# A transformer kernel on one core: first Q chunks by pairs of token tiles, Wq loaded behind four x tiles instead of eight, and two layernorms moved

## The chip, the cores and the metric

The kernel runs on one core of one Trainium2 chip. The metric is the device time of one execution in microseconds (us); lower is better. Each kernel was executed several times; beside every changed kernel, the kernel before was run on the same chip.

The engines: PE is the matmul engine, PEld its weight loads, DVE the vector engine, ACT the scalar engine, POOL the general one, SP the engine from which most transfers (DMA) are issued.

## The reference, cut to what matters

Four blocks in sequence on x of 2048 tokens by 1024: attention, feed-forward, attention, feed-forward, each with a layernorm in front and a residual.

```python
def _A_ref(x, wqkv, wo):            # H = 32 heads, Dh = 32, window W = 8, dilation 2
    qkv = ... (x @ wqkv) ...
    logits = einsum("bhsd,bhswd->bhsw", q, kg) * scale    # 8 earlier keys per token
    o = einsum("bhsw,bhswd->bhsd", softmax(logits), vg)
    return o @ wo
def _B_ref(x, w1, b1, w2, b2):
    return gelu(x @ w1 + b1) @ w2 + b2
x = x + _A_ref(_layernorm(x), ...)
x = x + _B_ref(_layernorm(x), ...)
# and both once more
```

## The kernel before

Tokens are worked in four groups of 512 (four tiles of 128 tokens each). For a group, Q, K and V are each made in 8 chunks of 8 matmuls of 512 columns. DVE multiplies Q by shifted K ("products") and adds them up in trees; PE sums over the heads ("head sum"); softmax; DVE multiplies by shifted V ("averaging"); PE applies wo. Between layernorm and Q the normalised tile `xn` has to be transposed into `xnT`: for the first group on PE, for later groups by a DMA transpose. The parts that the argument touches:

```python
wpool = ... bufs=5            # weight tiles of 1 MB; two make Wq, two Wk, two Wv
xn = lnp.tile(..., name="xn", bufs=3)

load_x(0)                     # four x tiles of 256 KB, on the SP queue
...
def ln_first():               # first group
    s = [ln_stats(0)]
    for tt in range(NTT):
        if tt + 1 < NTT:
            s.append(ln_stats(tt + 1))
        xn = ln_norm(tt, *s[tt])
        transpose_on_pe(xn, xa[0][:, tt, :, :])
        warm_up(4)            # matmuls on zeros, to keep the matmul clock up

def gen_qkv(n, ...):
    wq = load_qkv(0)
    wk = load_qkv(1)
    for c in range(6 if n == 0 else 0):           # first half of k for six chunks
        first[c] = qkv_chunk(wq, c, xnT, None, 0, KD // 2)
    for c in range(NCH):
        ps = ...                                  # rest of the chunk
        act.copy(qT[:, c, :], ps[:]); yield
    wv = load_qkv(2)                              # emitted after the last Q chunk
    ...                                           # 8 K chunks, then 8 V chunks

ln_first()
load_x(1)
stage(gen_qkv(0, 2), sides=at(0, ln_a, 1) + at(8, load_x, 2) + at(12, load_x, 3) + at(14, load_bias)
      + at(19, head_sum, 0, False))
q1 = gen_qkv(1, 2, defer=True, qk_pool=early)
stage(q1, sides=at(2, attend, 0) + at(2, spread, 0) + at(2, hold) + at(2, ln_a, 2, early) + ...)
...
stage(gen_ffn2(0), sides=at(15, hold) + ... + at(23, hold) + at(23, ln_a, 3))
```

`at(u, f, n)` emits f(n) after the u-th chunk of a stage. A scheduler then orders the instructions of each engine, and each engine runs its own in that order. `hold` keeps DVE work that is emitted later from being moved ahead of what was emitted before.

## Time and profile before

Median 1246.09 us (1245.93 to 1246.15, four runs): very steady.

| | value | where it is read |
|---|---|---|
| span | 1244.3 us | page |
| PE busy | 1233.5 us, 99% | page, part 1 |
| granted matmul clock | 1.000 | cores |
| spacing of 512-column matmuls | 216 ns | start to start, from the records |
| first real matmul | 14.22 us | timeline |
| PE waits after that | about 2.6 us in sum | timeline, start to start less 216 ns |

```profile
PE 1233.5 (99%) x5785; PEld 630.8 (51%) x5835; DVE 835.2 (67%) x864; ACT 305.7 (25%) x475; POOL 99.1 (8%) x215
```

This is part 1 of the page: busy time, share of the span and number of instructions. With PE at 99% there is little to win, and where it is shows in the timeline of PE. The columns are start, busy time, engine, line, operation, output and inputs, shape and number of merged instructions; in brackets the idle time before them and what ended it.

```profile
14.22 26.06 PE L118 MATMUL acc<-xnT,wt 128*128 128x512 bf16 x120 [0.34 <-ACT xnT L93]
...
49.12 0.62 PE L118 MATMUL L<-big,smat 128*32 128x512 bf16 x8
...
62.44 0.62 PE L118 MATMUL L<-big,smat 128*32 128x512 bf16 x8 [0.46 <-DVE big L93]
...
100.47 31.27 PE L118 MATMUL acc<-xnT,wt 128*128 128x512 bf16 x144 [0.75 <-ACT vT L93]
...
152.40 0.62 PE L118 MATMUL L<-big,smat 128*32 128x512 bf16 x8
...
258.83 1.89 PE L118 MATMUL acc<-wt,oT 128*128 128x512 bf16 x8 [0.47 <-DVE tmp L93]
...
260.96 8.79 PE L118 MATMUL acc<-wt,oT 128*128 128x512 bf16 x39 [0.24 <-DVE x L93]
...
269.68 0.62 PE L118 MATMUL L<-big,smat 128*32 128x512 bf16 x8
```

The `L` lines are head sums. There are four places with waits: the head until 14.22, the second head sum at 62.44 (DVE's products), the third group's Q at 100.47, and the second wo at 258 to 261. The wait at 100.47 is put down to ACT, but the third group's last DMA transpose lands at 100.34.

The next lines are the SP queue of the same kernel in the first Q stage. `wt` at 22.80 and 28.08 are the two halves of Wv; transposes and x tiles stand between them. From the landings in the trace, Wv's halves arrive at 30.21 and 36.74 us, and V starts on PE near 42 us.

```profile
22.80 0.57 SPq L93 DMA_DIRECT2D wt<-in_A_wqkv_dram  x1
23.46 2.05 SPq L93 DMA_TRANSPOSE xnT<-xn  x1
25.57 2.41 SPq L93 DMA_DIRECT2D x<-in_A_x_dram  x4
28.08 0.60 SPq L93 DMA_DIRECT2D wt<-in_A_wqkv_dram  x1
```

### The profile page before, as it was taken

The numbers are of one execution on the slowest core, as the hardware profiler recorded it, in microseconds if no ns is written. First come the engines' busy times: TensorE is split into PE (matmuls) and PEld (weight loads), VectorE is DVE, ScalarE is ACT, GpSimd is POOL, SyncE is SP. The second block draws the span as 40 slices with busy tenths as digits, with TensorE's granted clock in tenths as the row PEclk, the third lists the DMA queues.
The fourth block names the chain that finished last, engine by engine and source line by source line (L and its number), as shares of the span: only waits on it lengthen the run. The fifth ranks groups of instructions, "written<-read, shape, count | busy, mean of one in ns | idle before, by whom it ended". The sixth has DMA issues, their size and how long they took to land.

```text
span 1244.3 us, 13978 instructions
## 1 busy us (share of the span) xinstructions
PE 1233.5 (99%) x5785; PEld 630.8 (51%) x5835; DVE 835.2 (67%) x864; ACT 305.7 (25%) x475; POOL 99.1 (8%) x215
## 2 busy tenths in 40 slices
PE   9999999999999999999999999999999999999998
PEld 5666544446444564445644456444554444444444
DVE  4999989896995989527994379943598688012001
ACT  3333252013430134201351013410234101310310
POOL 3040010012001100101001010000000002000000
PEclk9999999999999999999999999999999999999999
DMA  9755564466846647555566575566754567546441
GB/s 284 253 190 169 152 208 148 161 174 207 212 135 203 169 149 206 185 170 148 177 176 197 165 176 170 163 195 197 192 161 140 182 203 179 181 157 194 148 138 53
DMA packets 215295, 219.81 MB, mean 177 GB/s; under 512 B 66034, under 2 KB 184960, under 8 KB 212160
## 3 DMA queue, kind: packets, MB, share of 16 engines
q1 hardware_dynamic: 212560, 208.16, 56.0%
q0 software_dynamic: 2672, 10.76, 2.7%
q8 instruction: 45, 0.74, 0.2%
q14 instruction: 18, 0.15, 0.0%
HBM read 197.40 MB, written 6.29 MB: 164 GB/s over the span
## 4 chain that ended last, share of the span: by engine, by line
PE 79%; issue 0%; DVE 0%; POOL 0%
PE acc L118 78%; PE L L118 0%; DVE x L93 0%; POOL rstd L93 0%; DVE xn L93 0%
## 5 line engine op out<-in xcount | busy, mean ns | idle before, releaser
L118 PE MATMUL acc<-xnT,wt 128*128 128x512 bf16 x3328 | 722.1, 379 | 1.1 <-ACT vT L93 0.8
L118 PEld LDWEIGHTS <-wt 128*128 128x128 bf16 x3328 | 394.8, 119 | 325.2 <-issue 5.3
L118 PE MATMUL acc<-wt,hT 128*128 128x512 bf16 (+1 forms) x1780 | 386.0, 376 | 2.1
L118 PEld LDWEIGHTS <-hT 128*128 128x128 bf16 x1820 | 178.1, 98 | 209.0
L93 DVE TENSOR_TENSOR big<-big 128x2048 bf16<-128x2048 bf16 (+2 forms) x182 | 240.3, 1349 | 1.8
L93 ACT ACTIVATE hT<-acc,b1T 128x512 bf16<-128x512 f32 x224 | 151.6, 687 | 318.4 <-PE acc L118 317.8
L93 DVE TENSOR_TENSOR big<-abc,vT 128x4096 bf16<-128x4096 bf16 x64 | 144.2, 2282 | 52.1 <-DMA abc<-a_d 52.1
L93 DVE TENSOR_TENSOR big<-qT,kT 128x4096 bf16<-128x4096 bf16 x64 | 143.9, 2286 | 31.4 <-ACT kT L93 30.5
L93 DVE TENSOR_TENSOR tmp<-acc,b2bc 128x512 f32<-128x512 f32 x56 | 38.6, 689 | 178.8 <-PE acc L118 175.4
L93 ACT CAST qT<-acc 128x512 bf16<-128x512 f32 x64 | 37.2, 587 | 332.8 <-PE acc L118 332.7
L118 PE MATMUL acc<-wt,oT 128*128 128x512 bf16 x440 | 97.7, 379 | 1.1 <-DVE tmp L93 0.5
L93 DVE BATCH_NORM_STATS2 stats<-x 128x6 f32<-128x512 bf16 x128 | 83.9, 677 | 3.3 <-DMA x<-in_A_x_dram 2.5
L118 PEld LDWEIGHTS <-oT 128*128 128x128 bf16 x448 | 43.9, 98 | 53.8 <-issue 1.3
L93 DVE TENSOR_TENSOR x<-acc,big 128x512 bf16<-128x512 f32 (+1 forms) x9 | 5.7, 632 | 90.0 <-PE acc L118 90.0
L93 POOL TENSOR_TENSOR rstd<-mv,eps_t 128x1 f32<-128x1 f32 x64 | 19.0, 297 | 502.1 <-DVE mv L93 502.1
L93 ACT CAST vT<-acc 128x512 bf16<-128x512 f32 x64 | 37.5, 586 | 84.7 <-PE acc L118 84.7
L93 DVE TENSOR_SCALAR xn<-x,mv,rstd 128x1024 bf16<-128x1024 bf16 x64 | 34.8, 543 | 35.0 <-POOL rstd L93 30.9
L93 ACT CAST kT<-acc 128x512 bf16<-128x512 f32 x64 | 37.4, 586 | 70.5 <-PE acc L118 70.5
L93 POOL DMA_DIRECT2D a_d<-a x32 | 19.6, 637 | 411.7 <-DVE a L93 411.7
L93 DVE TENSOR_TENSOR x<-acc,x 128x512 bf16<-128x512 f32 x64 | 42.8, 671 | 2.6 <-PE acc L118 2.3
L93 POOL TENSOR_TENSOR rstd<-rstd,mhalf 128x1 f32<-128x1 f32 x64 | 40.6, 634 | 5.0
L93 DVE TENSOR_TENSOR x<-tmp,x 128x512 bf16<-128x512 f32 x56 | 38.6, 689 | 1.5
(48 smaller groups left out, 207.7 us busy)
## 6 DMA issues: line engine op xcount, KB each, us to landing
wt<-in_B_w_dram SPq DMA_DIRECT2D x56, 1024.0 KB, 5.8
wt<-in_B_w_dram SPq DMA_DIRECT2D x64, 896.0 KB, 4.9
wt<-in_A_wqkv_dram SPq DMA_DIRECT2D x48, 1024.0 KB, 5.6
wt<-in_A_wo_dram SPq DMA_DIRECT2D x16, 1024.0 KB, 5.0
abc<-a_d POOLq DMA_DIRECT2D x32, 256.0 KB, 4.2
x<-in_A_x_dram SPq DMA_DIRECT2D x16, 256.0 KB, 6.2
out_dram<-x SPq DMA_DIRECT2D x31, 128.0 KB, 1.8
a_d<-a POOLq DMA_DIRECT2D x32, 64.0 KB, 3.6
```

Of the source, the lines that this page charges most:

```text
L93: inst = f(*args, **kwargs)
L118: return pe(nc.tensor.matmul(*args, **kwargs))
```

## The change

Its intent is to take away all four waits: start Q on two tiles instead of four and fetch Wq sooner (the head); do the third group's layernorm and transposes early, and the first group's attention later (the waits at 62 and 100 us); take the statistics of the fourth group's layernorm out of the crowded place at 250 us (the wait at 258). The text below calls the three parts head, middle and statistics.

```diff
 # head
+wq_first = load_qkv(0)                       # right behind the first four x tiles
 def ln_first():
-    ... four tiles normalised, transposed on PE, 4 warm-ups each
+    ... tiles 0 and 1 transposed on PE, copied in halves, 4 warm-ups in all;
+    ... tiles 2 and 3 only normalised, their transposes put in first_late
 # in gen_qkv
-for c in range(6 if n == 0 else 0):
-    first[c] = qkv_chunk(wq, c, xnT, None, 0, KD // 2)
+for kh in range(2 if n == 0 else 0):
+    for c in range(6):
+        first[c] = qkv_chunk(wq, c, xnT, first.get(c), kh * (KD // 2), (kh + 1) * (KD // 2), 0, 2)   # tiles 0, 1: 256 columns
+        if kh == 1 and c in (0, 3):
+            transpose_on_pe(*first_late.pop(0))
 ...                                           # then tiles 2, 3 of each chunk
 # middle
-stage(gen_qkv(0, 2), sides=at(0, ln_a, 1) + at(8, load_x, 2) + at(12, load_x, 3) + at(14, load_bias)
+stage(gen_qkv(0, 2), sides=at(0, load_x, 2) + at(0, ln_a, 1) + at(1, load_x, 3) + at(6, ln_a, 2, early) + at(14, load_bias)
-stage(q1, sides=at(2, attend, 0) + at(2, spread, 0) + at(2, hold) + at(2, ln_a, 2, early) + ...
+stage(q1, sides=at(6, attend, 0) + at(6, spread, 0) + at(6, hold) + ...
 # statistics
-stage(gen_ffn2(0), sides=at(15, hold) + ... + at(23, ln_a, 3))
+stage(gen_ffn2(0), sides=at(0, ln_stats_ahead, 3) + at(15, hold) + ... + at(23, ln_a, 3, None, True))
```

The order of the SP queue before: x of groups 0 and 1, Wq, Wk, three transposes, Wv first half, one transpose, x of group 2, Wv second half, x of group 3. After: x of group 0, Wq, x of group 1, Wk, x of group 2, three transposes, half of group 3's x, a transpose, the other half, three transposes of the third group, Wv first half, a transpose, Wv second half.

More of the change, by code (lines that the diff above doesn't have):

```diff
@@ L127, with load_qkv @@
     load_x(0)
+    def load_qkv(which):
+        tiles = []
+        for h in range(2):
+            wt = wpool.tile([P, KD // 2, D], BF16, name="wt")
+            sp.dma_start(wt[:], wqkv_v[:, h * (KD // 2):(h + 1) * (KD // 2), which * D:(which + 1) * D])
+            tiles.append(wt)
+        return tiles
+    wq_first = load_qkv(0)
     warm = bigp.tile([P, P], BF16, name="big")
@@ L145 @@
     b2bc = const.tile([P, D], BF16, name="b2bc")
+    mv_ahead = const.tile([P, NTT, 2], F32, name="mv_ahead")
+    rstd_ahead = const.tile([P, NTT, 1], F32, name="rstd_ahead")
     def build_constants():
@@ L165, in load_bias, with ln_stats @@
         act.copy(b1T[:], ps[:])
-    def ln_stats(t):
+    def ln_stats(t, mv=None, rstd=None, between=None):
         stats = lnp.tile([P, 2, 6], F32, name="stats")
@@ L171, in ln_stats @@
             vec.bn_stats(stats[:, h, :], x[t][:, h * HALF:(h + 1) * HALF])
-        mv = lnp.tile([P, 2], F32, name="mv")
+            if h == 0 and between is not None:
+                between()
+        if mv is None:
+            mv = lnp.tile([P, 2], F32, name="mv")
+            rstd = lnp.tile([P, 1], F32, name="rstd")
         vec.bn_aggr(mv[:], stats[:])
-        rstd = lnp.tile([P, 1], F32, name="rstd")
         pool.tensor_tensor(out=rstd[:], in0=mv[:, 1:2], in1=eps_t[:], op=ALU.add)
@@ L177, in ln_stats, with ln_stats_ahead @@
         return mv, rstd
+    def ln_stats_ahead(g):
+        for tt in range(NTT):
+            ln_stats(g * NTT + tt, mv_ahead[:, tt, :], rstd_ahead[:, tt, :])
     def ln_norm(t, mv, rstd):
@@ L182, in ln_norm, with transpose_on_pe @@
         return xn
-    def transpose_on_pe(xn, out):
-        pst = psum.tile([P, KD, P], BF16, name="acc", bufs=6)
+    def transpose_on_pe(xn, out, pst=None, halves=1):
+        if pst is None:
+            pst = psum.tile([P, KD, P], BF16, name="acc", bufs=6)
         for k in range(KD):
             pe(nc.tensor.transpose(pst[:, k, :], xn[:, k * P:(k + 1) * P], ident[:]))
-        act.copy(out, pst[:])
+        n = KD // halves
+        for h in range(halves):
+            act.copy(out[:, h * n:(h + 1) * n, :], pst[:, h * n:(h + 1) * n, :])
     late = []
@@ L194, in transpose_late, with ln_tile @@
             transpose_on_pe(*late.pop(0))
-    def ln_tile(t, tt, xnT, on_pe=False):
-        mv, rstd = ln_stats(t)
+    def ln_tile(t, tt, xnT, on_pe=False, ahead=False):
+        mv, rstd = (mv_ahead[:, tt, :], rstd_ahead[:, tt, :]) if ahead else ln_stats(t)
         xn = ln_norm(t, mv, rstd)
@@ L202, in ln_tile @@
         sp.dma_start_transpose(xnT[:, tt, :, :], xn[:].rearrange("s (k p) -> s k p", p=P))
+    first_late = []
     def ln_first():
@@ L207, in ln_first, with norm @@
         vec.on = True
-        s = [ln_stats(0)]
-        for tt in range(NTT):
-            if tt + 1 < NTT:
-                s.append(ln_stats(tt + 1))
-            xn = ln_norm(tt, *s[tt])
-            transpose_on_pe(xn, xa[0][:, tt, :, :])
-            warm_up(4)
+        both = psum.tile([P, 2, KD, P], BF16, name="L", bufs=1)
+        stats = {}
+        def norm(tt):
+            xn = ln_norm(tt, *stats.pop(tt))
+            if tt < 2:
+                transpose_on_pe(xn, xa[0][:, tt, :, :], halves=2)
+            else:
+                first_late.append((xn, xa[0][:, tt, :, :], both[:, tt - 2, :, :]))
+            if tt == 0:
+                warm_up(4)
+        stats[0] = ln_stats(0)
+        stats[1] = ln_stats(1)
+        norm(0)
+        stats[2] = ln_stats(2, between=lambda: norm(1))
+        stats[3] = ln_stats(3, between=lambda: norm(2))
+        norm(3)
         vec.on = False
@@ L227, with qkv_chunk @@
     xb = {}
-    def load_qkv(which):
-        tiles = []
-        for h in range(2):
-            wt = wpool.tile([P, KD // 2, D], BF16, name="wt")
-            sp.dma_start(wt[:], wqkv_v[:, h * (KD // 2):(h + 1) * (KD // 2), which * D:(which + 1) * D])
-            tiles.append(wt)
-        return tiles
-    def qkv_chunk(wts, c, xnT, ps=None, k0=0, k1=KD):
+    def qkv_chunk(wts, c, xnT, ps=None, k0=0, k1=KD, t0=0, t1=NTT):
         if ps is None:
@@ L240, in qkv_chunk @@
         for k in range(k0, k1):
-            mm(ps[:], lhsT=wts[k // (KD // 2)][:, k % (KD // 2), c::NCH], rhs=xnT[:, :, k, :], start=(k == 0), stop=(k == KD - 1))
+            mm(ps[:, t0 * P:t1 * P], lhsT=wts[k // (KD // 2)][:, k % (KD // 2), c::NCH], rhs=xnT[:, t0:t1, k, :],
+               start=(k == 0 and t0 == 0), stop=(k == KD - 1), skip_group_check=t1 - t0 < NTT)
         return ps
@@ L282, in gen_qkv @@
         qk_pool = qk_pool or attp
-        wq = load_qkv(0)
+        wq = wq_first if n == 0 else load_qkv(0)
         wk = load_qkv(1)
@@ L286, in gen_qkv @@
         first = {}
-        for c in range(6 if n == 0 else 0):
-            first[c] = qkv_chunk(wq, c, xnT, None, 0, KD // 2)
+        for kh in range(2 if n == 0 else 0):
[3 more added lines that the diff above has]
+                    transpose_on_pe(*first_late.pop(0))
         for c in range(NCH):
-            ps = qkv_chunk(wq, c, xnT, first[c], KD // 2) if c in first else qkv_chunk(wq, c, xnT)
+            ps = qkv_chunk(wq, c, xnT, first[c], t0=2) if c in first else qkv_chunk(wq, c, xnT)
             act.copy(qT[:, c, :], ps[:])
@@ L436, in warm_up, with ln_a @@
             mm(ps[:], lhsT=warm[:], rhs=warm[:].unsqueeze(1).to_broadcast([P, NTT, P]), start=True, stop=True)
-    def ln_a(n, pool=None):
+    def ln_a(n, pool=None, ahead=False):
         xa[n] = new_xnT(pool)
         for tt in range(NTT):
-            ln_tile((n % NG) * NTT + tt, tt, xa[n])
+            ln_tile((n % NG) * NTT + tt, tt, xa[n], ahead=ahead)
     def stage(gen, count=None, sides=()):
@@ L471 @@
         load_x(1)
-        stage(gen_qkv(0, 2), sides=at(0, ln_a, 1) + at(8, load_x, 2) + at(12, load_x, 3) + at(14, load_bias)
-              + at(19, head_sum, 0, False))
+        stage(gen_qkv(0, 2), sides=at(0, load_x, 2) + at(0, ln_a, 1) + at(1, load_x, 3) + at(6, ln_a, 2, early)
+              + at(14, load_bias) + at(19, head_sum, 0, False))
         q1 = gen_qkv(1, 2, defer=True, qk_pool=early)
-        stage(q1, sides=at(2, attend, 0) + at(2, spread, 0) + at(2, hold) + at(2, ln_a, 2, early) + each(new_prod, 1, 8, 1, 0, 4) + each(av, 0, 12, 1))
+        stage(q1, sides=at(6, attend, 0) + at(6, spread, 0) + at(6, hold) + each(new_prod, 1, 8, 1, 0, 4) + each(av, 0, 12, 1))
         q2 = gen_qkv(2, defer=True)
@@ L481 @@
     stage(gen_ffn1(0), sides=at(2, attend, 1) + at(2, spread, 1) + at(2, hold) + each(new_prod, 2, 2, 1, 0, 4) + each(av, 1, 6, 2))
-    stage(gen_ffn2(0), sides=at(15, hold) + each(new_prod, 2, 15, 1, 4, 8) + at(23, hold) + at(23, ln_a, 3))
+    stage(gen_ffn2(0), sides=at(0, ln_stats_ahead, 3) + at(15, hold) + each(new_prod, 2, 15, 1, 4, 8) + at(23, hold) + at(23, ln_a, 3, None, True))
     for n in range(1, N - 2):
```

## The prediction

> **What bounds it now.** TensorE. On the page PE is busy 1233.5 of 1244.3 us (99%) at a granted clock of 1.000; the chain of waits is almost all PE matmuls, 216 ns start to start. The change can only win time in which PE has no useful work. The timeline shows where that is:
> - the head: the first real matmul starts at 14.22 us, after four token tiles are normalised and transposed;
> - 62.4 us: 0.5 us, PE waits for the last product tree before the first group's attention sums (DVE works without a break from 30.6 to 62.4);
> - 99.3 to 100.5: 0.9 us; put down to ACT, but the third group's last DMA transpose lands at 100.34, so I read it as xnT being late;
> - 258.0 to 261.4: about 1.2 us, wo waits for accumulators that DVE has not emptied, because the fourth group's layernorm (250.3 to 259.7) stands before the adds.
>
> **The change, costed.**
> 1. Head. The first six Q chunks start on tiles 0 and 1. The second tile's normalise can follow at about 8.1, its half copies end near 10. Wq lies behind four x tiles, not eight. In the trace 256 KB takes 0.67 us and 1 MB 2.70 us once the queue is full, and landings keep the order of issue (the Trainium skill, "DMA: Bandwidth & Descriptors", "Queues, rings and completion order", has each engine consume its ring in order; the trace agrees). x3 lands at 6.80; Wq's halves then land near 9.5 to 10.2 and 12.2 to 12.9 (12.87 and 15.58 before). First real matmul about 10.2. Splitting 48 matmuls into 96 of 256 columns is almost free: 109 ns apiece in the last FFN. The wait for tile 3 (copied near 16.7) takes some back: Q ends near 25.4, not 28.0. Gain 2.6 us.
> 2. Given back. x4 to x11 and Wk now lie ahead of the DMA transposes, and the third group's layernorm stands before the products on DVE and waits for xn buffers that transposes free. Products start about 30.5, as before, with one normalise inserted: first tree about 47.3 (46.5 before), needed after the fourth V chunk, which PE reached at 48.8 before. Wv's second half lies behind transposes: I estimate it lands near 41 (36.74 before), 1 us after V wants it. Either way 1.3 us is lost: net 1.3 us at the first head sum.
> 3. Attention of group 0 moves four Q chunks later: removes the 0.5 us wait; DVE idles instead. The wait at 99.3 (0.9 us) goes. The averaging of V should still end about 129 us, when PE reaches wo (131.6 before): little slack.
> 4. Statistics ahead take about 6 us off DVE at 250 and put it near 180, before DVE's idle 4 us at 222: most of the 1.2 us at 258 goes.
> From there on nothing changes.
>
> **Sum:** 1.3 + 0.5 + 0.9 + 1.1 = 3.8 us: 1242.3 us, range 1240.0 to 1244.7. Faster by over 2%: 0.01; within 2%: 0.98; slower by over 2%: 0.01.
>
> **What would show it.** First 256-column matmul near 10.2; last Q copy near 26; PE gaps at the start of V (39.5) or the first head sum (46), 1 to 2 us in sum; none at the second sum, the third group's Q, or the second wo; every later stage shifted alike.
>
> **What would make it wrong.** Wq landing sooner (head gain 4 us); transposes landing later than 30 us, so that products and V both start late (gain near 1 us); PE's clock falling during the gap before 10 us; DVE late for wo.

## The result, and the profile after

Median 1248.39 us (1248.06 to 1249.75, four runs) against 1246.09: ratio 1.0021, 95% interval 1.0007 to 1.0035. Ratios here are the mean time of one kernel's runs over that of the other's of the same rounds, so not quite the ratio of the medians that are quoted. The change made the kernel about 2.3 us slower where 3.8 us less was predicted. The prediction is wrong.

```profile
PE 1236.3 (99%) x5871; PEld 633.3 (51%) x5871; DVE 836.2 (67%) x864; ACT 305.9 (25%) x477; POOL 95.2 (8%) x215
```

Part 1 of the page tells almost nothing: PE is as busy as before. PE's timeline tells more:

```profile
10.36 3.37 PE L118 MATMUL acc<-xnT,wt 128*128 128x256 bf16 x28 [1.45 <-DMA wt<-in_A_wqkv_dram]
...
17.04 20.94 PE L118 MATMUL acc<-xnT,wt 128*128 128x256 bf16 x120 [0.22 <-ACT xnT L93]
...
41.44 1.09 PE L118 MATMUL acc<-xnT,wt 128*128 128x512 bf16 x4 [1.46 <-DMA wt<-in_A_wqkv_dram]
45.03 8.66 PE L118 MATMUL acc<-xnT,wt 128*128 128x512 bf16 x28 [2.51 <-DMA wt<-in_A_wqkv_dram]
53.62 0.61 PE L118 MATMUL L<-big,smat 128*32 128x512 bf16 x8
...
155.49 0.61 PE L118 MATMUL L<-big,smat 128*32 128x512 bf16 x8
...
271.74 0.61 PE L118 MATMUL L<-big,smat 128*32 128x512 bf16 x8
```

The old waits are gone: no idle time at the second head sum, the third group's Q or the second wo. There are two new ones, both for `wt`, the halves of Wv, at the start of V. Then comes an odd line: 28 matmuls from 45.03 take 8.66 us, where at 216 ns they would take 6.

Set against the milestones before, the balance is (negative: the changed kernel is ahead):

| milestone | before | after | difference |
|---|---|---|---|
| first real matmul | 14.22 | 10.36 | -3.9 |
| last Q chunk copied (start of the copy) | 28.23 | 25.93 | -2.3 |
| first head sum | 49.12 | 53.62 | +4.5 |
| head sum of the second group (first part) | 152.40 | 155.49 | +3.1 |
| head sum after the second wo | 269.68 | 271.74 | +2.1 |
| end | 1244.3 | 1246.4 | +2.1 |

So everything is lost between 26 and 54 us (6.8 us), and the two old waits and the statistics win back 1.4 and 1.0 us, much as predicted.

Where did the 6.8 us go? The chain of waits has it (start, length, what ran or was waited for):

```profile
17.04 19.95 PE acc L118 x116
36.99 7.99 DMA wt<-in_A_wqkv_dram
44.99 0.05 issue
45.03 8.66 PE acc L118 x28
53.69 0.55 PE L L118 x8
```

Wv's second half is issued at 36.99 and lands at 44.99; before, it was issued at 28.08 and landed at 36.74. The SP queue shows why it is issued so late:

```profile
28.78 4.47 SPq L93 DMA_TRANSPOSE xnT<-xn  x3
33.31 0.85 SPq L93 DMA_DIRECT2D wt<-in_A_wqkv_dram  x1
34.25 2.65 SPq L93 DMA_TRANSPOSE xnT<-xn  x1
36.99 4.67 SPq L93 DMA_DIRECT2D wt<-in_A_wqkv_dram  x4
```

The four transposes of the third group stand around Wv, not wanted by PE before about 103 us in this kernel. SP issues in order, and in the first 60 us of every trace of this case its transfers also land in the order of issue, so Wv's halves wait behind those transposes. A rival reading is that SP itself was late, because a transpose in front of Wv has to wait for its normalise on DVE. The landings speak against it for the second half: it lands 2.73 us after the transpose before it (42.26), and 1 MB alone takes 2.70 us, so it came as soon as the transfers ahead of it were done. For the transfers before that this is not tested.

The odd line is the matmul clock. The windows view gives, for three stretches of the V stage, the length and busy time of each engine, then the granted clock (PEclk), the DMA share and GB/s. First before, then after:

```profile
42.50:45.00 2.50, 2.50 (x13) 1.65 (x12) 2.47 (x2) 1.56 (x4) 0.00 (x0) 1.00 0.84 256
45.00:48.50 3.50, 3.50 (x18) 2.34 (x17) 3.50 (x2) 1.17 (x2) 0.00 (x0) 1.00 1.04 397
48.50:52.00 3.50, 3.50 (x23) 1.91 (x22) 3.50 (x3) 0.94 (x2) 0.00 (x0) 1.00 0.07 24
```

```profile
42.50:45.00 2.50, 0.03 (x1) 0.00 (x0) 2.47 (x2) 0.00 (x0) 0.00 (x0) 0.63 1.05 388
45.00:48.50 3.50, 3.46 (x9) 1.39 (x10) 3.47 (x3) 0.58 (x1) 0.00 (x0) 0.50 1.05 386
48.50:52.00 3.50, 3.50 (x14) 1.92 (x13) 3.50 (x2) 0.58 (x1) 0.00 (x0) 0.79 1.06 390
```

In the middle stretch PE is "busy" in both, but it has 9 matmuls in it instead of 18, at a granted clock of 0.50. In the records the matmuls from 45.03 to 49.74 start 427 ns apart instead of 216: about twelve of them, 2.5 us more. The clock did not fall at 45 us but at 43.15, when 0.6 us of the second wait had passed (granted 1.00 from 42.5 to 43.1, 0.50 from 43.2 on), and it came back at about 49.98. The Trainium skill, "TensorE: Matmul & The Clock Gate", "Part 1: The HAM clock gate", says that an idle matmul array falls to half its clock and gets it back after some 3.4 us of sustained work; the trace agrees in kind, with 4.9 us of work (45.03 to 49.98) until it was back.

So far: 4.0 us of waits for Wv as the timeline counts them, and about 2.5 us of slow matmuls after them, 6.5 of the 6.8 us.

### The profile page after: what moved, and what is told of

It is laid out like the page before. It is cut to its first block, busy times and chain, and to the rows that moved or that the text cites. A ratio compares the mean times of both kernels' runs of the same rounds, so it can differ in the third digit from the quotient of the medians.

```text
span 1246.4 us, 14107 instructions
## 1 busy us (share of the span) xinstructions
PE 1236.3 (99%) x5871; PEld 633.3 (51%) x5871; DVE 836.2 (67%) x864; ACT 305.9 (25%) x477; POOL 95.2 (8%) x215
## 4 chain that ended last, share of the span: by engine, by line
PE 98%; DMA 1%; SPq 0%; ACT 0%; issue 0%; DVE 0%
PE acc L118 98%; DMA wt<-in_A_wqkv_dram 1%; PE L L118 0%; SPq L93 0%; ACT xnT L93 0%; PE L L206 0%; PE acc L206 0%; DVE x L93 0%
## 5 line engine op out<-in xcount | busy, mean ns | idle before, releaser
L118 PE MATMUL acc<-xnT,wt 128*128 128x512 bf16 (+1 forms) x3376 | 725.6, 377 | 5.6 <-DMA wt<-in_A_wqkv_dram 5.4
L93 DVE TENSOR_TENSOR big<-qT,kT 128x4096 bf16<-128x4096 bf16 x64 | 144.1, 2286 | 26.4 <-ACT kT L93 23.3
L93 POOL TENSOR_TENSOR rstd<-mv,eps_t 128x1 f32<-128x1 f32 x60 | 15.1, 251 | 501.4 <-DVE mv L93 501.4
L93 POOL TENSOR_TENSOR rstd<-rstd,mhalf 128x1 f32<-128x1 f32 x60 | 33.8, 563 | 4.7
```

Of the source, the lines that this page charges most:

```text
L93: inst = f(*args, **kwargs)
L118: return pe(nc.tensor.matmul(*args, **kwargs))
```

## The experiments

Theory T: the change as a whole puts Wv behind eight transposes and twelve x tiles on one queue, and the wait that this makes costs the clock too. Rivals: R1, DVE's products hold the stage, now that a third layernorm stands before them (then Wv's lateness only covers another wait); R2, the new head costs more than it wins (96 small matmuls, transposes amid the stage); R3, the low clock is no real loss. A later rival, T2, was that the bias broadcast disturbs the transposes.

### Wv ahead of the third group's transposes

```diff
-at(6, ln_a, 2, early)
+at(8, ln_a, 2, early)      # of the changed kernel: emitted after Wv's loads
```

> Changed kernel, but the third group's layernorm is emitted two chunks later, so that on the DMA queue both halves of Wv go ahead of its four transposes; DVE work the same. Theory T (Wv is late because it queues behind those transposes, and the wait also costs the matmul clock): Wv's second half lands near 37 us instead of 44.99, no PE wait at the start of V, no 427 ns matmuls at 45 to 50; a wait of about 1 us for the first product tree may show at the first head sum. Total near 1243 (1242.5 to 1243.7), under both kernels. Rival R1 (DVE's products, delayed by the layernorm before them, are what holds the stage; Wv only hides it): the head sum stays at about 53 us, total 1247 to 1248.4.

Measured: 1244.71 us (1242.98 to 1245.91), ratio to the kernel before 0.9988 (0.9973 to 1.0003). Wv landed at 35.71 and 39.97 us, there is no wait at V and no slow matmul in the profiled run, and the mean of the runs is 4.1 us under the changed kernel's. So Wv's place in the queue is the main cause. The sizes missed: the second half was expected near 37 us, and the median lies 1 us above the expected range; the profiled run is the fastest of four, and the slower ones have no profile. And R1 is not quite dead: the head sum now has a wait of its own, twice as long as expected.

```profile
37.49 8.85 PE L118 MATMUL acc<-xnT,wt 128*128 128x512 bf16 x40
48.52 0.61 PE L118 MATMUL L<-big,smat 128*32 128x512 bf16 x8 [2.18 <-DVE big L93]
```

DVE's products start at 31.62 here (30.58 in the kernel before), because the third group's normalises stand before them and wait for transposes to free `xn` buffers; one more normalise waits for a transpose that lands at 40.98, amid the first tree. In the changed kernel this second limit was hidden behind the wait for Wv. With only the first repaired, the second shows.

### Dummy matmuls in the wait

```diff
+if n == 0 and c == 0:
+    fill(7);  ps = qkv_chunk(wv, c, xnT, None, 0, KD // 2)
+    fill(11); ps = qkv_chunk(wv, c, xnT, ps, KD // 2)
```

> Changed kernel, with 7 dummy matmuls before the first V matmul and 11 before the first one that reads Wv's second half, to keep PE busy while it waits; nothing else moves. If the twelve matmuls at 427 ns after the wait (45.0 to 49.7 us) are a real loss, caused by PE's idleness: they become 216 ns, total lower by 2.4 us, 1246.0 (1245.7 to 1246.5), granted clock back to 1.000. Rival R3 (the low clock is only in the records, or comes from something else than idleness): no change, 1248.4.

Measured: 1247.31 us (1245.48 to 1249.77); the mean is 1.2 us under the changed kernel's, with ranges that overlap. PE's timeline of the profiled run:

```profile
42.61 1.09 PE L118 MATMUL acc<-xnT,wt 128*128 128x512 bf16 x4 [1.81 <-DMA wt<-in_A_wqkv_dram]
43.53 2.54 PE L118 MATMUL acc<-ident 128*128 128x512 bf16 x11
46.20 6.26 PE L118 MATMUL acc<-xnT,wt 128*128 128x512 bf16 x28
52.40 0.61 PE L118 MATMUL L<-big,smat 128*32 128x512 bf16 x8
```

The same 28 matmuls now take 6.26 us instead of 8.66: the 2.4 us are a real loss on PE, and idleness causes it, so R3 falls. That the total falls by 2.4 us, as expected, is not shown. As a total the run is inconclusive: Wv landed 1.2 us later in this run (46.16 instead of 44.99) and PE waited for that.

### The head alone

The kernel before, with only the head of the change.

> The head alone: Wq ahead of the x tiles, Q by pairs of token tiles, rest as in the kernel before. T: head gain of 2.3 us at the last Q copy; Wv lands in time as before; DVE's product chain starts 2 us earlier but not more, so the second head sum may still wait 0.5 to 0.9 us; the waits near 99 and 258 us stay. Total 1244.0 (1243.5 to 1244.5). Rival R2 (the split in 256 columns and the transposes amid the Q stage cost more than they win): no faster than 1246.

Measured: 1243.73 us (1243.62 to 1244.17), ratio 0.9982 (0.9965 to 0.9999), steady. R2 falls: the head wins what its milestone said, 2.3 us. The old waits stay:

```profile
59.99 0.61 PE L118 MATMUL L<-big,smat 128*32 128x512 bf16 x8 [0.47 <-DVE big L93]
...
98.05 31.27 PE L118 MATMUL acc<-xnT,wt 128*128 128x512 bf16 x144 [0.77 <-DMA xnT<-xn]
...
256.47 1.89 PE L118 MATMUL acc<-wt,oT 128*128 128x512 bf16 x8 [0.46 <-DVE tmp L93]
```

The middle line also supports the prediction's reading of the third group's wait: here the profile itself puts it down to the DMA transpose and not to ACT.

### V ordered by halves of k

```diff
+first = {}
+for c in range(5 if n == 0 else 0):
+    first[c] = qkv_chunk(wv, c, xnT, None, 0, KD // 2)     # then the second halves
```

> Changed kernel, with the V stage of the first group ordered as Q was before: the first half of k for five chunks, then the second half. Wv stays late. T: the 1.6 us wait for Wv's first half stays, the 2.7 us wait for its second half is covered by 20 matmuls, and with the short wait the clock does not fall, so another 2.4 us: total 1243.3 (1242.9 to 1244.2). Rival R1 (products on DVE hold the head sum): the wait moves to the head sum, total above 1246.

Measured: 1243.33, 1243.71, 1247.61 and 1247.98 us. Two runs are what T expected; the profiled one is of these, with a wait of 1.43 us for the first half, none for the second, and no slow matmuls. The two long runs have granted clocks of 0.997 and 0.999; no profile of them exists, so what happened in them is not shown. The median, 1245.66, is outside the expected range: the order helped in two runs of four, and doesn't make the kernel safe.

### The statistics alone

> The kernel before with the fourth group's statistics ahead and nothing else. T: the three waits of PE at 258 to 261 us (about 1.1 us in sum) go, nothing else moves: 1245.0 (1244.8 to 1245.3), as steady from run to run as the kernel before. Rival (the statistics delay V's averaging and a new wait appears at wo near 255): no faster than 1246.

Measured: 1244.87 us (1244.80 to 1244.89). As expected: 1.1 us.

### The middle part alone

The kernel before, with the x loads, the third group's layernorm and the attention placed as in the change.

> The kernel before with the middle part alone: x loads earlier, the third group's layernorm in the first Q stage, the first group's attention four chunks later; head and statistics as before. T: Wv's second half lands near 45 us instead of 36.74, V wants it near 42.8, so PE waits 2 to 3 us at the start of V (and some cold matmuls may follow); the waits at 62 and 99 us (1.4 us) go. Total 1247.5 (1246.3 to 1249), less steady from run to run than the kernel before. Rival R1 (the fault lies in the new head, which makes PE want everything too early): no more than 0.5 us of waiting at V, total 1244.7.

Measured: 1245.74 us (1245.68 to 1246.00), less harm than expected: T had 1246.3 at the least, with 2 to 3 us of waiting at V. Wv's second half landed at 44.09, V wanted it near 43, PE waited 0.9 us, no matmul was slow, and the two old waits (1.4 us) went. With the next run this has to be read with care.

### Middle and statistics, with the old head

> Changed kernel with the head of the kernel before (four whole tiles, Wq behind eight x tiles); middle and statistics as changed. T in its new form (the parts are nearly harmless one by one, and the new head and the middle part spoil each other: PE reaches V 2.3 us sooner, while the same bytes still stand ahead of Wv): one wait of about 1.1 us for Wv's second half, no cold matmuls, the sum of the two single runs, 1244.7 (1244.4 to 1245.1), steady; that is under the changed kernel by 3.7 us although its first real matmul starts 4 us later. Rival (the middle part and the statistics together do harm): 1246 or more.

Measured: 1246.84 us (1244.96 to 1249.25). The expectation failed. In the profiled run (1245.85) the wait for Wv was 1.9 us:

```profile
45.04 6.26 PE L118 MATMUL acc<-xnT,wt 128*128 128x512 bf16 x28 [1.95 <-DMA wt<-in_A_wqkv_dram]
```

Wv's second half landed at 44.99, exactly as in the changed kernel, although Wq was loaded at its old place. That much of theory T's new form holds: the bytes ahead of Wv are the same with either head, so Wv's landing doesn't move, and the new head only makes PE want it 2.3 us sooner. But the middle part is not harmless alone: with the statistics' 1.1 us added back it is worth between -0.2 us (the run above) and +1.8 us (this one). The two runs with a granted clock of 0.999 are the longest (1247.95 and 1249.25), which suggests slow matmuls there; they have no profile. DVE nearly held this run as well: its products started only at 35.48, because a normalise had waited 3.25 us for a transpose, and PE waited another 0.17 us for them at the head sum.

### The bias loads behind Wv

```diff
-pool.dma_start(b1_rows[:] ...); pool.dma_start(b2bc[:] ...)     at(14, load_bias)
+sp.dma_start(b1_rows[:] ...);   sp.dma_start(b2bc[:] ...)       at(22, load_bias)
```

> Changed kernel, with the two bias loads (7 KB and the 256 KB broadcast) issued from the sync queue behind Wv instead of from the pool queue at 29.8 us, amid the transposes. Theory T2 (the broadcast shares the DMA engines with the transposes and holds them up by 2 to 3 us, and that is a part of Wv's lateness): transposes 36.35 and 38.76 become about 34 and 35.2, Wv's halves land near 38 and 42, PE waits 1.5 us instead of 4.3 and its clock stays up: 1243.3 (1242.6 to 1244.8). Theory T alone (only the order of the queue counts): Wv earlier by 0.7 us, the time of 256 KB: 1247 to 1248.

Measured: 1248.66 us (1247.80 to 1249.45). T2 falls: with the broadcast out of the way, Wv still landed at 42.45 and 46.14. T alone missed here too: it expected Wv 0.7 us earlier and a total of 1247 to 1248, and the second half landed 1.1 us later than in the changed kernel. PE's timeline of this run has something else that the changed kernel doesn't have:

```profile
42.49 1.90 PE L118 MATMUL acc<-xnT,wt 128*128 128x512 bf16 x4 [2.94 <-DMA wt<-in_A_wqkv_dram]
46.19 7.83 PE L118 MATMUL acc<-xnT,wt 128*128 128x512 bf16 x28 [1.80 <-DMA wt<-in_A_wqkv_dram]
```

After one wait of 2.94 us already the first four matmuls are slow (1.90 us instead of 1.09), and eight of the next 28 are.

### A version that should beat both

The head and the statistics as changed, the x loads as before, the attention four chunks later, but the third group's layernorm held behind the first group's products:

```diff
-at(6, ln_a, 2, early)                      # in the first Q stage
+at(2, hold) + at(2, ln_a, 2, early)        # in the second group's stage, ahead of attend at 6
+extra[11] = early                          # one more xn buffer, for the group's last tile
```

The added buffer has a reason: with three, the last normalise would have waited on DVE, ahead of the attention, for a transpose that is queued behind weights. A fourth buffer in the shared pool did not fit in memory (a later pool wants 28 KB per partition, and 26.4 KB are left), so it lies in a pool that lives only in this stage.

> A version that should beat both: new head, statistics ahead, and attention of the first group four chunks later as in the changed kernel, but the third group's layernorm held until DVE has finished the first group's products (about 60 us), with one more buffer so that its last tile needn't wait for a transpose; x loads at their old places. T: Wv lands before 36 us, no wait at V, at either head sum, at the third group's Q or at the second wo: 1241.3 (1240.8 to 1241.9), steady within 0.3 us. Rival: DVE, with the layernorm before the attention, is late for wo near 129 us and gives back 1 to 3 us: 1242.5 to 1244.5.

Measured: 1241.14 us (1240.46 to 1243.01), ratio 0.9963 (0.9950 to 0.9975). The median is as expected, the spread is not.

### The same, with warm-up matmuls in the gap before Q

```diff
-if tt == 0:
+if tt < 2:
     warm_up(4)
```

> The version that beats both (e8), with four more warm-up matmuls after the second tile's transposes, in the 0.9 us in which PE waits for the copy and for Wq. If e8's spread from run to run (1240.5 to 1243.0, with the longer runs at a granted clock of 0.998 to 0.999) comes from this gap, where PE is idle just before real work, the spread shrinks to under 0.8 us and the median is 1240.7 (1240.3 to 1241.3). If the spread comes from elsewhere (a transfer's landing, or the wait at another place), median and spread stay as they are.

Measured: 1240.48 us (1240.36 to 1241.68, four of five within 0.25 us), ratio 0.9956 (0.9944 to 0.9969). This is the best version: 5.6 us under the kernel before, 7.9 us under the changed one. The spread shrank from 2.55 to 1.3 us, not to the 0.8 us expected; that the gap before Q was its source is not shown. Five runs of each are few, and the head alone has the same kind of gap (1.47 us) and varied by 0.55 us only. A transfer's landing stays a rival: in the profiled runs with the new head the first real matmul started between 9.58 and 10.81 us, most often when Wq had landed. PE in the same stretch:

```profile
9.58 3.35 PE L118 MATMUL acc<-xnT,wt 128*128 128x256 bf16 x28
...
37.23 8.86 PE L118 MATMUL acc<-xnT,wt 128*128 128x512 bf16 x40
46.01 0.61 PE L118 MATMUL L<-big,smat 128*32 128x512 bf16 x8
46.56 19.21 PE L118 MATMUL acc<-xnT,wt 128*128 128x512 bf16 x88
65.70 0.61 PE L118 MATMUL L<-big,smat 128*32 128x512 bf16 x8
```

No bracket with idle time stands behind any of them: V runs into both head sums without a wait. The first head sum is at 46.01, against 49.12 before and 53.62 after.

### All together

| kernel | median us | range | PE's wait for Wv in the profiled run |
|---|---|---|---|
| before | 1246.09 | 1245.93 to 1246.15 | none |
| changed | 1248.39 | 1248.06 to 1249.75 | 1.46 and 2.51, then slow matmuls |
| head alone | 1243.73 | 1243.62 to 1244.17 | none |
| statistics alone | 1244.87 | 1244.80 to 1244.89 | none |
| middle alone | 1245.74 | 1245.68 to 1246.00 | 0.9 |
| middle and statistics | 1246.84 | 1244.96 to 1249.25 | 1.95 (0.17 at the head sum) |
| changed, Wv ahead of transposes | 1244.71 | 1242.98 to 1245.91 | none (2.18 at the head sum) |
| changed, dummy matmuls | 1247.31 | 1245.48 to 1249.77 | 1.81 |
| changed, V by halves of k | 1245.66 | 1243.33 to 1247.98 | 1.43 |
| changed, bias behind Wv | 1248.66 | 1247.80 to 1249.45 | 2.94 and 1.80, slow matmuls |
| best version without the added warm-up | 1241.14 | 1240.46 to 1243.01 | none |
| best version | 1240.48 | 1240.36 to 1241.68 | none |

The three parts alone give -2.3, -1.1 and -0.2 us by their medians, each against the kernel before of its own rounds: -3.6 us in sum, near the predicted -3.8. Together they give +2.3 us. The difference of about 6 us arises at one place, the start of V. How it is to be shared among the parts stays open: middle and statistics without the new head were already 2.0 us over the sum of their single runs, with a range of 4.3 us.

## Why the prediction was wrong, point by point

1. **Head.** Right, but for 0.3 us. First 256-column matmul predicted near 10.2, measured 10.36; Wq's halves at 10.31 and 13.02 (predicted up to 10.2 and 12.9); last Q copy predicted near 26, measured 25.93; gain 2.3 us instead of 2.6. The split was nearly free: 109 ns apiece. The prediction had the landings keep the order of issue. The Trainium skill, "DMA: Bandwidth & Descriptors", "Queues, rings and completion order", says only that each DMA engine consumes its ring in order, and warns that completion need not keep the order of issue; on SP's queue the landings keep it here.
2. **"Wv's second half lies behind transposes: I estimate it lands near 41 ... Either way 1.3 us is lost."** This is the step that failed; all but 0.3 us of the 6.1 us of error lies in it. The mechanism (Wv behind transposes, PE waiting at V) was right, and the place (39.5 us) too. Two sizes were wrong. First, Wv's halves landed at 41.39 and 44.99, so that PE waited twice, 4.0 us in sum. I had costed a transpose at about 1.1 us, the distance of two landings in a quiet stretch of the trace before (22.54 and 23.62). In the changed kernel, from the landing of the first at 24.71 to that of the last at 42.26, there lie seven transposes, four x tiles, Wv's first half and the biases; with 0.67 us for an x tile and 2.70 us for the half, 12.2 us are left for seven transposes and the biases, about 1.7 us for each transpose if the biases took nothing. With the biases moved away the same sum gives 1.9 us, so they don't explain it. Within these 12.2 us lies about 1 us, just before Wv's first half landed, in which hardly anything moved (22 GB/s from 40 to 41 us; see the last point below). Second, the term of the clock was not in the sum at all, 2.5 us; I had named a falling clock as a danger only for the gap before 10 us. At the first head sum the kernel was thus 4.5 us late instead of 1.3 us early.
   The first tree of products was estimated well: products from 31.25 (30.5), tree done at 47.6 (47.3). It was no limit in the changed kernel, but became one when Wv was repaired.
3. **Attention later, third group's Q.** Right: the waits at 62 and 100 us went (from +4.5 to +3.1, 1.4 us, as predicted), and DVE's averaging was in time for wo, with no wait there.
4. **Statistics ahead.** Right: +3.1 to +2.1, and 1.1 to 1.2 us by itself.
5. **"From there on nothing changes."** Right: +2.1 at 271.74 and +2.1 at the end.

The prediction's own list of dangers had "transposes landing later than 30 us, so that products and V both start late (gain near 1 us)". It was the right danger, and still too small. The range, 1240.0 to 1244.7, left out the loss because I gave each cost one value and let the wait for Wv and the wait for the tree stand for each other; what a wait does to the speed of the work after it was left out.

## What to carry to other kernels

Work that is moved "into idle time" of one engine still takes a place in a queue of another; before moving a layernorm, list what its transfers will stand in front of, and when that is wanted. A PE wait can cost more than its length: after waits of 1.46 and 2.51 us, and in another run after one of 2.94 us, the next twelve matmuls took twice their time (2.5 us more), while after single waits of 1.95 and 2.18 us none did in the profiled runs. Dummy matmuls in the wait kept the clock up here, without a clear gain in the total; reordering the loads took the wait away. When several changes are made at once, time them one by one and together: here three parts that were each harmless or useful alone, in sum -3.6 us, were +2.3 us together, and the two good ones with a different placing of the third gave -5.6 us.

## What the Trainium skill lacked or had wrong

- "TensorE: Matmul & The Clock Gate", "Part 1: The HAM clock gate", gives one idle window of about 3.4 us as what drops the clock. Here no single wait was so long when it fell. In the changed kernel it fell at 43.15 us, after 1.46 us of idle, four matmuls (1.09 us) and 0.6 us of idle; in the run with the biases moved at 42.6, after one wait of 2.94 us. Single waits of 1.95 and 2.18 us did not drop it in the profiled runs. It gives about 3.4 us of sustained work for the way back, and around 4 us, 0.5 more or less, in an example; here 4.9 us passed from 45.03 and, in the other run, 3.2 us from 46.19. The time at half clock was 6.8 us in both. A sentence on a window that is idle in part only would help.
- "DMA: Bandwidth & Descriptors", "Rules for kernel authors", says that a transpose next to ordinary DMAs "needs nothing". For correctness perhaps; for time it doesn't say what a transpose costs the transfers beside it, and no page was found that does (some rate the transpose itself). From 26 to 43 us the queues moved 5.34 MB in the kernel before (no transpose issued within the stretch, one issued at 23.46 still served in it) and 4.30 MB in the changed one (five issued). The two stretches differ in more than transposes (in the kernel before, the queues had little to do at the end), so this is no clean measure of the cost. The DMA view of that stretch says, first before, then after:

```profile
DMA packets 3712, 5.34 MB, mean 314 GB/s; under 512 B 1232, under 2 KB 1232, under 8 KB 3712
```

```profile
DMA packets 7024, 4.30 MB, mean 253 GB/s; under 512 B 5660, under 2 KB 5674, under 8 KB 7022
```

- No page has this: in the packet records of the run with the biases moved, from 40.15 to 42.2 us, 19 packets of 256 bytes (those of a transpose) lasted 2.0 us each, where 18 ns is the rule, while a single stream of 2048-byte packets of 84 ns each went on, one every 80 ns. The same stands in the changed kernel (20 packets of 1.3 us from 39.82) and, behind Wv's first half as well, in the kernel before (14 of 1.1 to 1.6 us from 28.48), so it is no feature of the new order. It looks as though one of the DMA engines was behind with Wv's first half and the others waited for it inside the transpose; no run tests that, and it stays open. It could be a part of why a transpose costs more among weights than alone, and of why Wv's landing varied between 44.1 and 46.2 us in the kernels that share this queue order.
